# An attention and gating kernel: p v multiplies p's low part last, and z1 of the drain takes its PSUM banks from another pool

## The chip, the core and the metric

The kernel runs on one core of a Trainium2 chip. The metric is the device time of one execution in microseconds (us). Three executions of the kernel before took 1812.85, 1814.95 and 1819.16 us, so their median is 1814.95 us. One further execution was profiled. It took 1814.89 us, and its span from the first to the last instruction is 1813.1 us.

## What is computed

The reference, cut to what matters here (all of it in float32):

```
xn = layernorm(x)                                  # 2048 x 512
q  = (xn @ wq) as 32 heads of 128
s  = softmax(q @ k.T / sqrt(128)) @ v @ wo         # k, v: the last 512 cached rows of each head
z  = gelu(xn @ w_in)                               # 1376 columns: z1 is the first 688, z2 the rest
z2 = layernorm(z2)
g  = silu((z1 * (w_sp @ z2 + b_sp)) @ w_out)
out = x + s * g
```

Each product in it is made of three products: an operand a is held as a high part ah and a low part al = a - ah, both in the format float32r, and a b is computed as ah bh + ah bl + al bh, summed in PSUM.

## The kernel before

**Stages.** A short opening normalises the first rows and makes the first z1 products. Then comes the main loop (from about 50 to 1410 us of the span), which goes over 32 heads in two halves of the rows. After it a drain of some 40 us finishes the last blocks and makes the z1 products that are left. Then follow the z2 products, and from about 1510 us on the mixing by w_sp and the output projection.

**The main loop.** One block b is one head with 512 rows of x. It has four steps of 128 rows, so NBLK = 128 blocks make NSTEP = 512 steps. The work is software-pipelined by hand: in step t the code issues the scores of step t, the product p v of step t - 13 (PL, line 35 of the constants), and the output projection of step t - 18 (OL), along with the products for q of later blocks. The order in which the code issues instructions is the order on every engine, and each engine takes its own in that order.

For one step TensorE does this, in this order:

- the score (`score`, lines 470 to 479): three multiplications into a PSUM tile `ps_3` of the pool `ps_step`. VectorE takes its row maximum (line 477), and ScalarE the exponential (line 479). VectorE then turns p in pieces of 32 x 32 (line 488), and after four steps SyncE sends the block to DRAM and back (lines 492 and 500), which completes the transposition.
- the products for q (line 450), up to three of them, into `ps_a` of the pool `ps_acc`.
- p v (`pv`): p's transposed piece comes as `pT_h` and `pT_l` from `shares`. ScalarE makes the high part (line 507), and then GpSimd makes the low part by a subtraction (line 59, called in line 508). A block's four pieces are summed in one tile `ps_a`, which ScalarE and VectorE turn into `oT_h` and `oT_l` when the fourth is in (`pv_out`).
- the output projection (`outp`, lines 526 to 538): three multiplications into a `ps_3`, which VectorE adds to `sacc` (line 536).

`shares` runs two steps ahead of `pv`, and `pT_h` and `pT_l` have four buffers each. In the program's traces `wh` and `wl` are the high and low part of v (also of k and wo), and `ps` is `ps_3`.

The helper that issues three multiplications; the first operand is the one whose weights are loaded into the array:

```
    def mm3(ps, first, last, lhs, rhs):
        (lh, ll), (rh, rl) = lhs, rhs
        nc.tensor.matmul(ps, lh, rh, start=first, stop=False)      # line 65
        nc.tensor.matmul(ps, lh, rl, start=False, stop=False)      # line 66
        nc.tensor.matmul(ps, ll, rh, start=False, stop=last)       # line 67
```

In `pv` the first operand is v and the second is p. So the second multiplication, line 66, is the one that needs `pT_l`.

**The drain.** The z1 products of rows 8 to 15 (of 16 tiles of rows; T8 is 8) are spread over the last steps by the table DRAIN: first the eight with n = 0, at steps 505, 507, 509, 510, 511, 512, 513 and 514, then those with n = 1. Each is 12 multiplications of 344 columns, issued behind the step's output projection. ScalarE copies the result out of PSUM and issues its store to DRAM on its own queue (`z1_out`, lines 361 and 362). This copy's target has two buffers. In the drain the odd ones of the last subtractions for the split of w_in and for `pT_l` run on VectorE.

**PSUM.** There are eight banks. `ps_step` has four, named `ps_3`, and `ps_acc` has four, named `ps_a`. A new tile waits for the last reader of the tile that had its bank. Before, the z1 products with n = 0 take a `ps_3`, so scores, output projections and z1 share four banks; those with n = 1 take a `ps_a`.

**The SyncE queue.** SyncE issues nearly all DMAs, in the order of the code, and an issue that waits holds back those behind it. DMAs share eight semaphores. A DMA can be issued only when the one that had its semaphore before it has landed, whoever issued that one. In the drain this couples SyncE's loads with ScalarE's stores of z1. The loads of two blocks of x for the next stage (`fetch_x`, line 262, 1 MB each) stand there too.

Of the kernel before, what the change touches and what calls it, by code (L numbers as in the profile page):

```python
# [8 lines left out]
F32 = mybir.dt.float32  # L9
# [8 lines left out]
P = 128  # L18
# [16 lines left out]
T8 = NT // 2  # L35
# [5 lines left out]
def mixer_kernel(ctx: ExitStack, tc: tile.TileContext, x, wh, w_in, w_sp, b_sp, w_out, out):  # L41
# [8 lines left out]
    nc = tc.nc  # L50
# [12 lines left out]
    def mm3(ps, first, last, lhs, rhs):  # L63
        (lh, ll), (rh, rl) = lhs, rhs
        nc.tensor.matmul(ps, lh, rh, start=first, stop=False)  # L65
        nc.tensor.matmul(ps, lh, rl, start=False, stop=False)  # L66
        nc.tensor.matmul(ps, ll, rh, start=False, stop=last)  # L67

    def cols(pair, lo, hi):
        return tuple(t[:, lo:hi] for t in pair)  # L70
# [12 lines left out]
    ps_acc = psum.enter_context(tc.tile_pool(name="ps_acc", bufs=4, space=PSUM))  # L83
    ps_step = psum.enter_context(tc.tile_pool(name="ps_step", bufs=4, space=PSUM))
# [12 lines left out]
    raw, wt = {}, {}  # L97
# [241 lines left out]
    def zmm(ps, i, n, cs):  # L339
        for c in cs:  # L340
            mm3(ps, c == 0, c == NC - 1, tuple(x_op(i, a, c) for a in range(2)), cols(wt[("w", n), c], 0, NB))
# [8 lines left out]
                             start=k == 0, stop=k == len(order) - 1)  # L350

    def z1_product(i, n, between=lambda: None):
        ps = ps_acc.tile([P, 512], F32, name="ps_a") if n else ps_step.tile([P, 512], F32, name="ps_3")
        zmm(ps[:, :NB], i, n, range(2))
        between()
        zmm(ps[:, :NB], i, n, range(2, NC))
        return ps
# [6 lines left out]
    def z1_piece(i, n, between=lambda: None):  # L364
        z1_out(i, n, z1_product(i, n, between))


    qps, qT, pps, pD, pL, pT, oT, prob, sums = {}, {}, {}, {}, {}, {}, {}, {}, {}

    def where(b):  # L370

        w, r = divmod(b, NBLK // 2)
        p, k = divmod(r, 4)
        return w * H + 2 * p + k // 2, 2 * w + (0, 1, 1, 0)[k]
# [136 lines left out]
    def pv(b, c):  # L511
        if c == 0:
            pps[b] = ps_acc.tile([P, 512], F32, name="ps_a")
        mm3(pps[b], c == 0, c == 3, cols(wt[("h", where(b)[0]), 2], c * P, (c + 1) * P), pT.pop((b, c)))

    def pv_out(b, c):
        if c == 3:
# [85 lines left out]
    n, t = 0, 28  # L603
# [47 lines left out]
    ps = ps_step.tile([P, 512], F32, name="ps_3")  # L651
# [9 lines left out]
    ps = ps_step.tile([P, 512], F32, name="ps_3")  # L661
# [4 lines left out]
    ps = ps_acc.tile([P, 512], F32, name="ps_a")  # L666
# [18 lines left out]
    for t in range(T0, T1):  # L685
# [9 lines left out]
        i = t + XL  # L695
# [17 lines left out]
        if 0 <= bp < NBLK:  # L713
            pv(bp, cp)
        if 0 <= bo < NBLK:
            outp(bo, jo)
        if t in DRAIN:
            ps = z1_product(*DRAIN[t])
# [17 lines left out]

    split_piece(("w", 2), 3, nc.vector)
    ps = z1_product(*LAST[-1])
    split_piece(("w", 3), 1, nc.vector)
    z1_out(*LAST[-1], ps)  # L740
# [80 lines left out]
    with ExitStack() as st:  # L821
        pl = st.enter_context(tc.tile_pool(name="p2", bufs=1, reuse_waits="tile"))
# [193 lines left out]
```

## Time and profile before

| what | value |
|---|---|
| three timed executions | 1812.85, 1814.95, 1819.16 us |
| the profiled execution | 1814.89 us, span 1813.1 us |
| granted TensorE clock, mean | 0.998 |
| TensorE busy | 1793.2 us (99% of the span), 8658 multiplications |
| weight loads of TensorE | 1538.0 us (85%), 8658 |
| VectorE, ScalarE, GpSimd busy | 1395.4, 1174.4, 1237.8 us (77%, 65%, 68%) |
| DMA engines, main queue | 70.1% of 16 engines' span |

How to read the profile: PE is TensorE's multiplication and PEld its weight load, DVE is VectorE, ACT ScalarE, POOL GpSimd, SP SyncE. SPq and ACTq are DMA issues. A row of a timeline has the start in us, the duration in us, the engine, the line of the code, the operation, and output<-inputs; in brackets stands how long the engine was idle before it, and what ended that. Rows of multiplications overlap, since each is shown with its latency: the distance from start to start is what one costs. A view of waits has the waiting engine, its output tile and line, what it waited for, and then the us in total, the times, and the longest.

### The profile page before, as it was taken

How to read it: one execution, taken by the hardware profiler on the slowest of the kernel's cores; microseconds unless marked ns; L12 is line 12 of the kernel's file. 1: busy time of each engine (PE TensorE's matmuls, PEld its weight loads, DVE VectorE, ACT ScalarE, POOL GpSimd, SP SyncE). 2: the span in 40 equal slices, each digit the busy share in tenths (PEclk: the TensorE clock that was granted, in tenths of full speed). 3: DMA queues.
4: the chain of work that ended last, by engine and by line, in shares of the span. 5: the costliest groups of instructions: out<-in, count | busy, mean ns of one | idle time of the engine just before them, and what ended most of it. 6: DMA issues, size and time to landing. Idle time of an engine off the chain costs nothing.

```text
span 1813.1 us, 28712 instructions
## 1 busy us (share of the span) xinstructions
PE 1793.2 (99%) x8658; PEld 1538.0 (85%) x8658; DVE 1395.4 (77%) x2369; ACT 1174.4 (65%) x2625; POOL 1237.8 (68%) x1179
## 2 busy tenths in 40 slices
PE   8999999999999999999999999999999999999999
PEld 7887888888888888788888888888887999999998
DVE  5688988989898988888888888888888556433333
ACT  4777777777777777677777777777776444433332
POOL 2798898898888988788888888888887343000000
PEclk9999999999999999999999999999999999999999
DMA  5578887888888889787777777777778625554532
GB/s 181 176 226 249 245 252 236 266 251 232 253 254 248 250 248 303 256 256 226 232 219 223 219 230 221 225 235 218 226 224 253 219 86 172 171 172 148 182 118 92
DMA packets 181804, 394.07 MB, mean 217 GB/s; under 512 B 24368, under 2 KB 54832, under 8 KB 164496
## 3 DMA queue, kind: packets, MB, share of 16 engines
q1 hardware_dynamic: 177040, 386.60, 70.1%
q10 hardware_dynamic: 4608, 5.64, 0.9%
q8 instruction: 68, 1.11, 0.3%
q14 instruction: 88, 0.72, 0.1%
HBM read 225.42 MB, written 166.72 MB: 216 GB/s over the span
## 4 chain that ended last, share of the span: by engine, by line
PE 89%; DMA 6%; DVE 1%; ACT 1%; POOL 1%; issue 1%; SPq 1%; ACTq 0%; DVEq 0%; POOLq 0%
PE ps_a L450 14%; PE ps L67 12%; PE ps L65 12%; PE ps L66 12%; PE ps_a L66 7%; PE ps_a L67 7%; PE ps_a L65 7%; PE ps_g L65 4%; PE ps_g L67 4%; PE ps_g L66 4%; DMA p_dram<-pL 2%; DMA pL<-p_dram 1%; PE ps_f L67 1%; PE ps_f L65 1%; PE ps_f L66 1%
## 5 line engine op out<-in xcount | busy, mean ns | idle before, releaser
L59 POOL TENSOR_TENSOR pT_l<-pL,pT_h 128x512 fp32r<-128x512 f32 x507 | 656.5, 1298 | 187.6 <-ACT pT_h L507 155.4
L479 ACT ACTIVATE prob<-ps,nm 128x512 f32<-128x512 f32 x512 | 353.9, 691 | 330.4 <-DVE nm L477 320.8
L536 DVE SCALAR_TENSOR_TENSOR sacc<-ps,sums,sacc 128x512 f32<-128x512 f32 x496 | 369.6, 746 | 124.7 <-PE ps L67 118.8
L450 PE MATMUL ps_a<-x,x 128*128 128x512 f32 x1302 | 376.0, 389 | 1.0 <-DVE oT_l L59 1.0
L488 DVE STREAM_TRANSPOSE pL<-prob 128x512 f32<-128x512 f32 x512 | 358.7, 701 | 6.8 <-ACT prob L479 6.8
L477 DVE TENSOR_REDUCE nm<-ps 128x1 f32<-128x512 f32 x512 | 340.0, 664 | 7.0 <-PE ps L67 6.8
L507 ACT CAST pT_h<-pL 128x512 fp32r<-128x512 f32 x512 | 318.2, 622 | 28.1 <-DMA pL<-p_dram 7.6
L450 PEld LDWEIGHTS ps_a<-x,x 128*128 128x128 f32 x1302 | 244.4, 188 | 52.5 <-PE ps_a L450 1.8
L59 POOL TENSOR_TENSOR wl<-raw,wh 128x512 fp32r<-128x512 f32 x186 | 241.3, 1297 | 11.1 <-ACT wh L144 11.1
L66 PE MATMUL ps_a<-pT_l,wh 128*128 128x512 f32 x512 | 200.1, 391 | 3.0 <-POOL pT_l L59 2.8
L65 PE MATMUL ps_a<-pT_h,wh 128*128 128x512 f32 x512 | 199.5, 390 | 1.5 <-ACT pT_h L507 1.4
L65 PE MATMUL ps<-wh,qT_h 128*128 128x512 f32 x512 | 200.3, 391 | 0.5 <-DVE sacc L536 0.5
L67 PE MATMUL ps<-wh,qT_l 128*128 128x512 f32 x512 | 199.8, 390 | 0.0
L67 PE MATMUL ps_a<-pT_h,wl 128*128 128x512 f32 x512 | 199.3, 389 | 0.0
L66 PE MATMUL ps<-wl,qT_h 128*128 128x512 f32 x512 | 199.3, 389 | 0.0
L65 PE MATMUL ps<-wh,oT_h 128*128 128x512 f32 x512 | 199.3, 389 | 0.0
L66 PE MATMUL ps<-wl,oT_h 128*128 128x512 f32 x512 | 199.2, 389 | 0.0
L67 PE MATMUL ps<-wh,oT_l 128*128 128x512 f32 x512 | 199.2, 389 | 0.0
L67 PE MATMUL ps_g<-z_h,x 128*128 128x344 f32 x512 | 161.8, 316 | 0.0
L65 PE MATMUL ps_g<-z_h,x 128*128 128x344 f32 x512 | 161.8, 316 | 0.0
L66 PE MATMUL ps_g<-z_l,x 128*128 128x344 f32 x512 | 161.8, 316 | 0.0
L59 POOL TENSOR_TENSOR x<-wq,x 128x256 fp32r<-128x256 f32 x186 | 138.1, 743 | 1.5 <-ACT x L432 1.5
(203 smaller groups left out, 3179.4 us busy)
## 6 DMA issues: line engine op xcount, KB each, us to landing
p_dram<-pL SPq DMA_DIRECT2D x128, 1024.0 KB, 5.3
pL<-p_dram SPq DMA_DIRECT2D x256, 192.0 KB, 3.8
raw<-wh SPq DMA_DIRECT2D x188, 256.0 KB, 6.5
pL<-p_dram SPq DMA_DIRECT2D x256, 128.0 KB, 3.7
pL<-p_dram SPq DMA_DIRECT2D x256, 64.0 KB, 3.5
wq<-wh SPq DMA_DIRECT2D x62, 256.0 KB, 4.7
x<-w_sp SPq DMA_DIRECT2D x60, 256.0 KB, 5.7
x_dram<-rawx SPq DMA_DIRECT2D x32, 256.0 KB, 6.1
```

The source lines that it names most:

```text
L59: engine.tensor_tensor(lo, whole, hi.bitcast(F32), op=OP.subtract)
L65: nc.tensor.matmul(ps, lh, rh, start=first, stop=False)
L66: nc.tensor.matmul(ps, lh, rl, start=False, stop=False)
L67: nc.tensor.matmul(ps, ll, rh, start=False, stop=last)
L450: nc.tensor.matmul(qps[g, bank], wt["q", g, k][a][:, c * P:(c + 1) * P], X[g * 2 // H][ORDER[k]][:, b, c], start=first, stop=r == 5, skip_ ...
L477: nc.vector.tensor_reduce(nm, ps, axis=AX.X, op=OP.max, negate=True)
L479: nc.scalar.activation(prob[t], ps, AF.Exp, bias=nm, accum_out=sums[b][:, j:j + 1])
L488: nc.vector.transpose(pL[b][:, :, j * P:j * P + P].rearrange("p a (c q) -> p a c q", q=Q), prob.pop(t).rearrange("p (a c q) -> p a c q", a ...
L507: nc.scalar.copy(h, p)
L536: nc.vector.scalar_tensor_tensor(at, ps, rs, at, op0=OP.mult, op1=OP.add)
```

## The change

It has two parts. `pv` no longer calls `mm3`: it multiplies v high by p high, then v low by p high, then v high by p low, so that p's low part is needed by the third multiplication in place of the second. And `z1_product` takes a tile `ps_a` of `ps_acc` for n = 0 too, where the row tile is one of 8 to 15, that is, in the drain. The number of multiplications, weight loads and other instructions that compute is the same.

```
     def z1_product(i, n, between=lambda: None):
-        ps = ps_acc.tile([P, 512], F32, name="ps_a") if n else ps_step.tile([P, 512], F32, name="ps_3")
+        ps = ps_acc.tile([P, 512], F32, name="ps_a") if n or i >= T8 else ps_step.tile([P, 512], F32, name="ps_3")
...
     def pv(b, c):
         if c == 0:
             pps[b] = ps_acc.tile([P, 512], F32, name="ps_a")
-        mm3(pps[b], c == 0, c == 3, cols(wt[("h", where(b)[0]), 2], c * P, (c + 1) * P), pT.pop((b, c)))
+        (vh, vl), (ph, pl) = cols(wt[("h", where(b)[0]), 2], c * P, (c + 1) * P), pT.pop((b, c))
+        nc.tensor.matmul(pps[b], vh, ph, start=c == 0, stop=False)
+        nc.tensor.matmul(pps[b], vl, ph, start=False, stop=False)
+        nc.tensor.matmul(pps[b], vh, pl, start=False, stop=c == 3)
```

On TensorE a step of the main loop then stands as follows (the piece of the difference with the waits of each; `ps_a` is first the accumulator of q, then that of p v, `wh_811` and `wl_812` are v's parts):

```order
 L450 MATMUL ps_a<-x_508,x_751 128x512 x3
-L65 MATMUL ps_a<-pT_h,wh_811 128x512 [waits Activation_49]
-L66 MATMUL ps_a<-pT_l,wh_811 128x512 [waits Pool_49]
-L67 MATMUL ps_a<-pT_h,wl_812 128x512
+L515 MATMUL ps_a<-pT_h,wh_811 128x512 [waits Activation_49]
+L516 MATMUL ps_a<-pT_h,wl_812 128x512
+L517 MATMUL ps_a<-pT_l,wh_811 128x512 [waits Pool_49]
 L65 MATMUL ps_1012<-wh_747,qT_h 128x512
```

The wait for GpSimd's `pT_l` moved behind one more multiplication; nothing else on TensorE moved in the step.

On GpSimd the order stays, but waits change. A piece of its list of subtractions in the main loop:

```order
-L59 TENSOR_TENSOR pT_l<-pL,pT_h 128x512 [waits Activation_49]
+L59 TENSOR_TENSOR pT_l<-pL,pT_h 128x512 [waits PE_49,Activation_49]
 L59 TENSOR_TENSOR wl_1183<-raw,wh_1182 128x512 [waits DMAHW5_49,Activation_49]
 L59 TENSOR_TENSOR pT_l<-pL,pT_h 128x512 [waits PE_49,Activation_49]
 L423 TENSOR_TENSOR wq<-wq 128x256 [waits Pool_49]
 L59 TENSOR_TENSOR pT_l<-pL,pT_h 128x512 [waits PE_49,Activation_49]
-L59 TENSOR_TENSOR wl_1254<-raw,wh_1253 128x512 [waits DMAHW4_49,PE_49,Activation_49]
+L59 TENSOR_TENSOR wl_1254<-raw,wh_1253 128x512 [waits DMAHW4_49,Activation_49]
```

`pT_l`'s old content is now read by the last multiplication of p v, so a subtraction that before needed no wait of its own for TensorE has one. That is so for 182 of the 507, and in 155 places the wait is an instruction of its own; 60 subtractions `wl` lose such a wait.

In the drain, TensorE's list around step 509: the step's output projection (tile 17625), its z1 product (tile 17630), and the score of step 510 (tile 17660). Before:

```order
L65 MATMUL ps_3_17625<-wh3_17282,oT_h_17453 128x512 [waits Activation_49]
L66 MATMUL ps_3_17625<-wl3_17283,oT_h_17453 128x512
L67 MATMUL ps_3_17625<-wh3_17282,oT_l_17454 128x512
L65 MATMUL ps_3_17630<-x8_17180,x8_8451 128x344 [waits DVE_49]
...
L65 MATMUL ps_3_17660<-wh1_17312,qT_h_17366 128x512 [waits Activation_49]
```

And of the change:

```order
L65 MATMUL ps_3_17625<-wh3_17282,oT_h_17453 128x512 [waits Activation_49]
L66 MATMUL ps_3_17625<-wl3_17283,oT_h_17453 128x512
L67 MATMUL ps_3_17625<-wh3_17282,oT_l_17454 128x512
L65 MATMUL ps_a_17630<-x8_17180,x8_8451 128x344
...
L65 MATMUL ps_3_17660<-wh1_17312,qT_h_17366 128x512 [waits DVE_49]
```

The z1 product has no wait any more. The wait for VectorE is now at the score of the next step, and it is the same one: both tiles wait until VectorE has added the output projection of step 508 (tile 17594) to `sacc`, since both get its bank. On SyncE one more thing differs in the drain, since the order in which DMAs share the eight semaphores shifts. Of the first two loads of line 262, the first waited for a load of `pL` and the second for the landing of a z1 store that ScalarE had issued; in the changed program the first waits for the z1 store before that one, and the second for a load of `pL`.

## The prediction

> **What bounds the kernel now.** I read the page first, for which engine is full.
>
> ```profile
> span 1813.1 us, 28712 instructions
> PE 1793.2 (99%) x8658; PEld 1538.0 (85%) x8658; DVE 1395.4 (77%) x2369; ACT 1174.4 (65%) x2625; POOL 1237.8 (68%) x1179
> PE 89%; DMA 6%; DVE 1%; ACT 1%; POOL 1%; issue 1%; SPq 1%; ACTq 0%; DVEq 0%; POOLq 0%
> ```
>
> TensorE is busy 99% of the span and carries 89% of the chain that ended last. Neither part of the change takes a multiplication away, so the change can only give back time in which TensorE stands still: 1813.1 - 1793.2 = 19.9 us in all, much of it in the opening, which the change does not touch. What it waits for is in the view of waits, for the multiplications and for the weight loads ahead of them:
>
> ```profile
> PE ps_a L66 <- POOL pT_l L59: 2.8, 4, 0.8
> PE ps L65 <- DVE sacc L536: 2.1, 3, 1.6
> ...
> PEld ps_a L66 <- POOL pT_l L59: 6.4, 9, 1.3
> ```
>
> The first and the last row are the waits at which the new order of p v aims: nine times in 512 pieces the low part came too late for its weight load, and four of these left the multiplier idle by the profile. The second row holds one long wait of 1.6 us; the timeline below puts it on a z1 product. So before any detail the two parts have something like 2.8 to 6.4 us and 1.6 us to work on, 0.2 to 0.4% of the time.
>
> The price of one multiplication comes from a stretch of the timeline without a wait, first and last of nine in a row:
>
> ```profile
> 1396.92 0.39 PE L65 MATMUL ps<-wh,qT_h 128*128 128x512 f32 x1
> ...
> 1398.74 0.39 PE L67 MATMUL ps<-wh,oT_l 128*128 128x512 f32 x1
> ```
>
> Eight distances take 1398.74 - 1396.92 = 1.82 us, 0.2275 us each.
>
> **Part 1: p's low part last.** Where the low part is late at TensorE, 0.2275 us of work that does not need it is now done in the meantime. So an episode of waiting shrinks by at most 0.2275 us, and nine episodes give at most 2.05 us. But what one episode gives need not last. The first five lie close together:
>
> ```profile
> 77.90 0.19 PEld L66 LDWEIGHTS ps_a<-pT_l,wh 128*128 128x128 f32 x1 [0.48 <-POOL pT_l L59]
> ...
> 93.34 0.19 PEld L66 LDWEIGHTS ps_a<-pT_l,wh 128*128 128x128 f32 x1 [0.49 <-POOL pT_l L59]
> 76.50:95.90 19.40, 18.10 (x74) 13.28 (x74) 15.21 (x27) 14.32 (x34) 19.22 (x18) 1.00 0.83 255
> 95.90 0.62 ACT L507 CAST pT_h<-pL 128x512 fp32r<-128x512 f32 x1 [2.72 <-DMA pL<-p_dram]
> 101.05 0.19 PEld L450 LDWEIGHTS ps_a<-x,x 128*128 128x128 f32 x1 [0.56 <-PE ps_a L450]
> ```
>
> The third row is one of the table by stretches; its columns are the length of the stretch and the busy time of PE, PEld, DVE, ACT and POOL: GpSimd works 19.22 of 19.40 us. Its subtractions end when they end, and TensorE meets the last of them at 93.34 whatever it gained at the first. So these five give 0.2275 us together, not five times that. The last row shows TensorE waiting again at 101.05, now for a bank; its release goes through ScalarE, which the row ahead of it shows waiting 2.72 us for a DMA until 95.90. If that DMA is no earlier, the 0.2275 us are given back there. The later episodes look alike:
>
> ```profile
> 734.48 0.19 PEld L66 LDWEIGHTS ps_a<-pT_l,wh 128*128 128x128 f32 x1 [1.15 <-POOL pT_l L59]
> 741.12 0.19 PEld L65 LDWEIGHTS ps<-wh,qT_h 128*128 128x128 f32 x1 [0.21 <-ACT qT_h L384]
> 741.85 0.19 PEld L67 LDWEIGHTS ps<-wh,qT_l 128*128 128x128 f32 x1 [0.43 <-DVE qT_l L59]
> ```
>
> Here the low part stalls TensorE for 1.15 us, and 7 us later the parts of q do, which hang on ScalarE and not on TensorE's lead. A lead lasts only where every later wait is paced by TensorE itself, as a transfer that it started earlier. There are four such groups (77 to 93, 142.7, 734.5 and 1385.8 us), so part 1 gives between 0 and 4 x 0.2275 = 0.9 us by this reading, 2.05 us if no episode's gain is lost. I take 0.2 us, one group's worth, nearest to the rows that show it given back.
>
> What it adds: 182 subtractions on GpSimd now wait for TensorE, 155 of them by an instruction of its own. The buffer in question was read two steps earlier, so that wait is over when it is asked. Its price in GpSimd's queue is read from a `wl`, which has such extra waits already, behind a `pT_l`:
>
> ```profile
> 79.23 1.29 POOL L59 TENSOR_TENSOR pT_l<-pL,pT_h 128x512 fp32r<-128x512 f32 x1
> 80.47 1.29 POOL L59 TENSOR_TENSOR wl<-raw,wh 128x512 fp32r<-128x512 f32 x1
> 81.72 0.74 POOL L59 TENSOR_TENSOR x<-wq,x 128x256 fp32r<-128x256 f32 x1
> ```
>
> It starts 1.24 us after the `pT_l`, and the `x` behind it 1.25 us later: back to back either way. I take 0. The upper end is 0.05 us, the hop from VectorE's end at 1400.66 to TensorE's start at 1400.72 in the rows further down; that is 0.25 us for the five episodes in the full stretch and nothing elsewhere, since GpSimd is 68% busy. It would only eat part 1's gain.
>
> One rule speaks against the new order. The Trainium skill's page "TensorE: Matmul & The Clock Gate", section "Step-by-step: what each phase is for", says that weights are loaded apart from multiplying so that one load can serve many multiplications. By that rule the old order, with v's high part twice in a row, needs two loads for three multiplications, and the new one three. The page's row above has 8658 loads for 8658 multiplications, so the old order loads it again as well.
>
> **Part 2: z1 of the drain.** The wait of 1.6 us has this chain, rows of ScalarE, VectorE and TensorE in the order of time; the first two are an earlier z1 product, which waits for nothing, and the score behind it:
>
> ```profile
> 1393.05 0.32 PE L65 MATMUL ps<-x,x 128*128 128x344 f32 x1
> ...
> 1394.88 0.39 PE L65 MATMUL ps<-wh,qT_h 128*128 128x512 f32 x1
> ...
> 1396.67 0.33 ACTq L362 DMA_DIRECT2D z_dram<-z  x1
> 1397.57 0.47 ACT L144 CAST x<-rawx 128x344 fp32r<-128x344 f32 x1
> 1398.08 1.33 DVE L59 TENSOR_TENSOR x<-rawx,x 128x344 fp32r<-128x344 f32 x1 [3.46 <-ACT x L144]
> 1399.33 0.68 DVE L477 TENSOR_REDUCE nm<-ps 128x1 f32<-128x512 f32 x1
> 1399.93 0.73 DVE L536 SCALAR_TENSOR_TENSOR sacc<-ps,sums,sacc 128x512 f32<-128x512 f32 x1
> 1400.72 0.43 PE L65 MATMUL ps<-x,x 128*128 128x344 f32 x1 [1.59 <-DVE sacc L536]
> 1402.72 0.39 PE L65 MATMUL ps<-wh,qT_h 128*128 128x512 f32 x1
> ```
>
> ScalarE's store of an earlier z1 was held until 1396.67, VectorE stood idle for 3.46 us behind it, and so it emptied the output projection's bank only at 1399.93 + 0.73 = 1400.66. The z1 product of step 509 needed that bank. TensorE's last multiplication before it started at 1398.74, so without the wait the z1 product starts at 1398.74 + 0.23 = 1398.97. Twelve multiplications of 344 columns take 1402.72 - 1400.72 = 2.00 us in this execution but 1394.88 - 1393.05 = 1.83 us in the first two rows, where nothing waits. So they end at 1398.97 + 1.83 = 1400.80. What is late next: the score of step 510 now waits for the very release that z1 waited for, at 1400.66, which is when its weights are wanted. The hop of 0.06 us to 1400.72 costs it hardly anything; I put it at 1400.82. It started at 1402.72, so part 2 gives 1402.72 - 1400.82 = **1.9 us**. Bounds: 0, if the wait moves on whole, and 2.1 us, if the other waits of that row (2.1 - 1.6 = 0.5 us) go too, of which the nearest to 1.9 is what the rows sum to.
>
> ```profile
> 1403.00:1455.00 52.00, 52.00 (x288) 47.68 (x287) 27.20 (x43) 23.25 (x50) 16.34 (x15) 1.00 0.70 233
> ```
>
> This row of the table by stretches shows that TensorE had no gap from 1403 to 1455 us. Is there slack for it to come 1.9 us earlier? The transfers that feed p there are held by the z1 stores, which follow TensorE and move with it. So I let the whole 1.9 us reach the end; the stages behind have no wait that the profile shows for TensorE.
>
> **Sum.** 1.9 + 0.2 = 2.1 us. The profiled execution took 1814.89 us, which lies 0.06 us under the median of the three, so the forecast is 1814.9 - 2.1 = **1812.8 us**, 0.12% faster. A measurement of this kernel can tell about 0.3% (5.4 us) from no change, and the three runs are 6.3 us apart, so this counts as the same.
>
> **The rivals.** (a) Part 1's gains all last, because the transfers start earlier too: 1814.9 - 1.9 - 2.05 = 1810.9 us. For it speaks that the chain has only 6% of DMA; against it the rows at 101.05 and 741.12. (b) The stall of the drain comes back elsewhere. It starts with a landing that took long: the z1 store ahead of the held one landed only 7.0 us after its issue, where the median of these stores is 2.9:
>
> ```profile
> z_dram<-z ACTq DMA_DIRECT2D x1, 172.0 KB, 7.0
> z_dram<-z ACTq DMA_DIRECT2D x32, 172.0 KB, 2.9
> ```
>
> If it lands a microsecond or two later in another execution, the score of step 510 waits for it in full, and if it lands soon there was no stall to remove. Either way: 1814.9 - 0.2 = 1814.7 us. (c) Slower: the second load of 1 MB at line 262 starts together with the first one instead of 8 us behind it, and both crowd a z1 store.
>
> ```profile
> SPq L262 <- DMA z_dram<-z: 7.9, 1, 7.9
> z_dram<-z ACTq DMA_DIRECT2D x1, 172.0 KB, 7.8
> 1431.76 0.33 ACTq L362 DMA_DIRECT2D z_dram<-z  x1
> 1439.67 0.45 ACT L361 COPY z<-ps_a 128x344 f32<-128x344 f32 x1 [1.96 <-DMA z_dram<-z]
> 1440.52 0.62 ACT L507 CAST pT_h<-pL 128x512 fp32r<-128x512 f32 x1 [0.41 <-ACT z L361]
> 1443.40 0.39 PE L65 MATMUL ps_a<-pT_h,wh 128*128 128x512 f32 x1
> ```
>
> The store issued at 1431.76 landed 7.8 us later, at 1439.56, beside one such load. ScalarE waits for it before the next copy of z1, and ends the last block's `pT_h` at 1440.52 + 0.62 = 1441.14, 1.6 us after the landing. TensorE wants it at 1443.40, or 1.9 us earlier now, at 1441.50, and the store goes out at 1429.86. So it decides at a landing of 1441.50 - 1.6 - 1429.86 = 10.0 us. If two loads double the landing to 15.6 us, TensorE waits 5.6 us there: 1814.9 - 2.1 + 5.6 = 1818.4 us, slower. Against it: one more store, issued beside two such loads, landed in 7.6 us.
>
> ```profile
> 1452.52 0.33 ACTq L362 DMA_DIRECT2D z_dram<-z  x1
> x<-x_dram SPq DMA_DIRECT2D x2, 1024.0 KB, 6.5
> z_dram<-z ACTq DMA_DIRECT2D x1, 172.0 KB, 7.6
> ```
>
> The Trainium skill's page "DMA: Bandwidth & Descriptors", section "Queues, rings and completion order", says that a DMA engine goes round the queues that have work, a packet at a time; by that rule a store on ScalarE's queue is not put behind a second load on SyncE's, and the forecast stands. The two landings, 7.8 and 7.6 us, agree with it. (d) Weights that stand in the array already are cheap, so that the new order pays one weight load more for each of 512 pieces, at most 188 ns each (96 us): 1911 us. The equal counts of loads speak against it, and so do the equal distances within the nine multiplications above, in which a load of the same weights and of new ones alternate.
>
> **How the numbers follow.** Forecast 0.57, (a) 0.14, (b) 0.18, (c) 0.10, (d) 0.01. The predicted time is the forecast's, 1812.8 us. The cases (a) to (c) span 1810.9 to 1818.4 us, and the three runs lie from 2.1 us under their median to 4.2 us over it; a median of runs moves by about half of that. So the range is 1809.3 to 1818.4 us. Faster by over 0.3% (under 1809.5 us) needs (a) and a low draw: 0.06. Slower by over 0.3% (over 1820.4 us) needs (c) and a high draw, or (d): 0.06. The same: 0.88.
>
> **What would show it.** Part 1: the row of PEld waiting for `pT_l` (now at line 517) falls from 6.4 us by some 0.2 us an episode and does not vanish, and bank waits do not shrink. Part 2: TensorE's wait of 1.6 us for VectorE before a z1 product is gone, the score behind it starts at most 0.1 us late, and the drain is 1.9 us shorter from the z1 product of step 509 on. (b) would show as a wait of a score for VectorE of over 1 us in the drain, (c) as a wait of p v for ScalarE near 1441 us, (d) as distances over 0.2275 us at lines 515 to 517. Wrong I would be if another wait grew that the profile of before does not hold, as one of GpSimd for TensorE.

## The result, and the profile after

The changed kernel took **1813.65 us** (median of 19 executions, 1811.26 to 1816.47); the kernel before, beside it, 1816.28 us (19 executions, 1812.85 to 1821.64). The ratio is 0.9986, with a 95% interval of 0.9980 to 0.9992: faster by 1.5 to 3.6 us, 0.14%, and under the 0.3% within which the prediction counts a time as the same. The forecast was 1812.8 us, 0.12% under the profiled execution; that execution, at 1814.89 us, was itself 1.4 us under the median that before has now.

The page of the changed kernel, its span, its engines and its chain:

```profile
span 1810.6 us, 28863 instructions
PE 1793.3 (99%) x8658; PEld 1539.5 (85%) x8658; DVE 1395.6 (77%) x2369; ACT 1173.4 (65%) x2625; POOL 1237.7 (68%) x1179
PE 93%; DMA 4%; DVE 1%; POOL 1%; issue 1%; ACT 0%; SPq 0%; ACTq 0%; POOLq 0%; DVEq 0%
```

TensorE is as busy as before (1793.3 us), in a span that is 2.5 us shorter. The 151 more instructions are the waits on GpSimd (155 more, and a few fewer elsewhere), and GpSimd's busy time did not move. TensorE carries 93% of the chain in place of 89%, transfers 4% in place of 6%. The view of waits, weight loads, two rows of the change and one of before:

```profile
PEld ps_a L517 <- POOL pT_l L59: 4.7, 7, 1.3
PEld ps L65 <- DVE sacc L539: 2.1, 5, 0.8
```

```profile
PEld ps L65 <- DVE sacc L536: 3.6, 4, 2.0
```

The waits for `pT_l` fell from 6.4 to 4.7 us and those of a score or z1 for VectorE from 3.6 to 2.1 us. That looks like 1.7 + 1.5 us, and like the forecast. But only the second number stands up.

**The drain.** Timeline of the changed kernel around the z1 product of step 509, ScalarE's first two stores of the drain ahead of it:

```profile
1388.79 0.33 ACTq L362 DMA_DIRECT2D z_dram<-z  x1
1396.09 0.33 ACTq L362 DMA_DIRECT2D z_dram<-z  x1
1397.92 0.39 PE L67 MATMUL ps<-wh,oT_l 128*128 128x512 f32 x1
1398.15 0.32 PE L65 MATMUL ps_a<-x,x 128*128 128x344 f32 x1
...
1399.84 0.31 PE L67 MATMUL ps_a<-x,x 128*128 128x344 f32 x1
1400.12 0.19 PEld L65 LDWEIGHTS ps<-wh,qT_h 128*128 128x128 f32 x1 [0.25 <-DVE sacc L539]
1400.13 0.50 PE L65 MATMUL ps<-wh,qT_h 128*128 128x512 f32 x1
```

The second store went out 7.30 us behind the first, 0.08 us after the first had landed (1396.01); in before it was 7.07 us. The z1 product no longer feels it: it starts 0.23 us behind the last multiplication of the output projection. The score of step 510 now waits for VectorE, and it starts 1400.13 - 1399.84 = 0.29 us behind the last z1 multiplication in place of 0.15: 0.14 us late. Behind the drain the execution is 1.7 us further ahead of before than it was ahead of the drain.

**The main loop.** Start of the same multiplication of TensorE, in before, and how much earlier (-) or later it starts in other executions, worked out from their timelines (us):

| mark in before | 29.0 | 61.3 | 95.3 | 157.0 | 731.3 | 750.6 | 1380.7 | 1407.3 | last, 1808.7 |
|---|---|---|---|---|---|---|---|---|---|
| before, second profile | -1.0 | -1.0 | -0.7 | -2.7 | -2.0 | -0.6 | -0.6 | -1.1 | -1.1 |
| the change | +0.8 | +0.8 | +0.9 | -2.1 | -2.0 | -0.8 | -0.8 | -2.5 | -2.5 |
| the change, second profile | +0.6 | +0.6 | +1.1 | +0.5 | +0.6 | +2.5 | +2.5 | +0.5 | +0.5 |

Between 95 and 157 us the change gains 2.9 us and at 731 to 751 us it loses 1.3 us, and neither belongs to it: at the first place its own second profile gains 0.6 us, and the second profile of *before* gains 2.0; at the second all three lose, by 1.3 to 2.0 us, and in all three, but not in the first profile of before, TensorE's clock was halved for a while there (last section). Only the step from 1380.7 to 1407.3 us is the same wherever the banks are changed: -1.7 and -2.0, against -0.5 for the kernel before against itself. So the 2.5 us between the two profiled executions, so close to the 2.1 of the forecast, are a sum of terms of up to 3 us that cancelled by chance.

### The profile page after: what moved, and what is told of

Same layout as the page of the kernel before. It is cut to its first block, busy times and chain, and to the rows that moved or that the text cites. A ratio compares the mean times of both kernels' runs of the same rounds, so it can differ in the third digit from the quotient of the medians.

```text
span 1810.6 us, 28863 instructions
## 1 busy us (share of the span) xinstructions
PE 1793.3 (99%) x8658; PEld 1539.5 (85%) x8658; DVE 1395.6 (77%) x2369; ACT 1173.4 (65%) x2625; POOL 1237.7 (68%) x1179
## 4 chain that ended last, share of the span: by engine, by line
PE 93%; DMA 4%; DVE 1%; POOL 1%; issue 1%; ACT 0%; SPq 0%; ACTq 0%; POOLq 0%; DVEq 0%
PE ps_a L450 15%; PE ps L65 12%; PE ps L67 12%; PE ps L66 12%; PE ps_a L517 6%; PE ps_a L515 6%; PE ps_a L516 6%; PE ps_g L67 4%; PE ps_g L66 4%; PE ps_g L65 4%; PE ps_a L67 2%; PE ps_a L66 2%; PE ps_a L65 2%; DMA p_dram<-pL 1%; DMA pL<-p_dram 1%; PE ps_f L67 1%
```

## The experiments

Ratios are to runs of the kernel before on the same chip, with 95% intervals. They are not the quotients of the two medians, from which they differ by up to 0.0009. Each run was also profiled once.

**1. `order_only`: the new order of p v, the old banks** (the change without its first edit).

> Only the new order of p v, the drain as before. Theory of the prediction: an episode of waiting for pT_l shrinks by up to 0.2275 us and most of that is given back at the next wait, so about 0.2 us less than before (ratio 0.9999), the wait of 1.6 us of the z1 product at 1400 us stays, the pT_l waits of PEld fall from 6.4 to about 4.7 us. Rival: all gains last, 2.05 us less (ratio 0.9989). Second rival, from the trace of the change: TensorE is 2.0 us ahead of before at 146 us, so the order would be worth some 2.9 us there by starting transfers of p earlier.

Measured: 1816.97 us against 1816.03, ratio 1.0004 (0.9992 to 1.0017). Waits of this kernel, and its timeline in the drain:

```profile
PEld ps_a L517 <- POOL pT_l L59: 7.4, 10, 1.3
```

```profile
1390.32 0.35 ACTq L362 DMA_DIRECT2D z_dram<-z  x1
1395.81 0.45 ACT L361 COPY z<-ps 128x344 f32<-128x344 f32 x1 [1.09 <-PE ps L67]
1396.28 0.33 ACTq L362 DMA_DIRECT2D z_dram<-z  x1
1400.33 0.43 PE L65 MATMUL ps<-x,x 128*128 128x344 f32 x1 [0.48 <-DVE sacc L539]
```

The order alone has more waiting for `pT_l` than before (7.4 us, ten times), not less: three episodes came in, near 166, 720 and 723 us, that before does not have. The lower end of the interval, -1.5 us, excludes rival (a) with its 2.05 us, and the second rival with its 2.9 us too. This profile does gain 2.4 us between 95 and 157 us, but `before_again` and `low_first`, with other orders, gain 2.0 us there. And the stall of z1 is here, but with 0.48 us in place of 1.59. The second store was not held at all: the first had landed at 1395.83, and the second went out right behind its copy (1395.81 + 0.45 = 1396.26), 5.96 us behind the first. So part of the stall needs no late landing.

**2. `banks_only`: the new banks, the old order.**

> Only the z1 banks of the drain, p v's order as before. Theory of the prediction: the wait of 1.6 us before the z1 product of step 509 is gone, the score behind it waits at most 0.1 to 0.2 us, 1.9 us less than before (ratio 0.9990). Rival: the wait moves to the score, 0 us (ratio 1.000).

Measured: 1814.43 us against 1816.03, ratio 0.9991 (0.9980 to 1.0002), so the timing alone does not tell it from no change. In the trace the stall is gone: with the stores 1402.76 - 1396.16 = 6.60 us apart the z1 product follows the output projection by 0.23 us.

```profile
1396.16 0.33 ACTq L362 DMA_DIRECT2D z_dram<-z  x1
1402.76 0.34 ACTq L362 DMA_DIRECT2D z_dram<-z  x1
...
1405.30 0.39 PE L67 MATMUL ps<-wh,oT_l 128*128 128x512 f32 x1
1405.53 0.32 PE L65 MATMUL ps_a<-x,x 128*128 128x344 f32 x1
```

One wait is new, and it is close to rival (c), but small: p v of the last block waits 0.24 us, behind a `pT_h` for which ScalarE had waited 2.34 us until 1438.68. That wait was for a load of `pL`, which landed at 1438.54 beside the two loads of 1 MB issued at 1436.29 and 1436.77, and not for a z1 store. Weight loads of the same run:

```profile
1440.71 0.19 PEld L66 LDWEIGHTS ps_a<-pT_l,wh 128*128 128x128 f32 x1 [0.50 <-POOL pT_l L59]
```

**3. `low_first`: the dose the other way.** p's low part first, old banks:

```
-        mm3(pps[b], c == 0, c == 3, ...)
+        nc.tensor.matmul(pps[b], vh, pl, start=c == 0, stop=False)
+        nc.tensor.matmul(pps[b], vh, ph, start=False, stop=False)
+        nc.tensor.matmul(pps[b], vl, ph, start=False, stop=c == 3)
```

> The dose the other way: p's low part is multiplied first, so it is needed one multiplication sooner than before. If every episode's time counts in full, each of the nine grows by 0.2275 us and others join them: at least 2.05 us more than before (ratio at least 1.0011), pT_l waits of PEld at least 8.4 us. If the time is mostly given back at the next wait, the waits grow as much but the time by some 0.2 to 1 us (ratio up to 1.0005).

Measured: 1817.13 us against 1816.03, ratio 1.0004 (0.9993 to 1.0016). Its waits:

```profile
PEld ps_a L515 <- POOL pT_l L59: 9.5, 11, 3.0
```

The waits grew by 3.1 us over before, but one of them, 3.0 us at the half's boundary, now holds the wait for `pT_h` too. The time is compatible with either reading; the first group, below, is not.

**4. `low_late`: a larger dose.** For c < 3 the multiplication vh pl is kept in a list and issued behind the step's output projection (old banks).

> A larger dose: for three of a block's four pieces the low part is multiplied behind the output projection, four or more multiplications (0.9 us) later than before. Waits for pT_l should nearly vanish (under 2 us of PEld's 6.4). If their time is kept, 4 to 5 us less than before (ratio 0.997 to 0.998). If what paces these stretches is GpSimd's own work and the landing of p's transfers, the waits turn into waits for banks, pT_h or q and the time falls by under 2 us (ratio 0.999 to 1.000).

Measured: 1813.93 us against 1816.03, ratio 0.9990 (0.9978 to 1.0001).

```profile
PEld ps_a L518 <- POOL pT_l L59: 3.4, 4, 1.3
```

Less waiting, but not "nearly none". The expectation overlooked that steps 13 to 17, where most of the first group lies, have no output projection yet, so the dose there is that of the change. The time cannot be told from no change.

**5. `store_pool`: no hold of ScalarE.** The kernel before, with the z1 stores of the drain issued by GpSimd:

```
-        nc.scalar.dma_start(z1_dram[:, i, n * NB:(n + 1) * NB], z)
+        (nc.gpsimd if i >= T8 else nc.scalar).dma_start(z1_dram[:, i, n * NB:(n + 1) * NB], z)
```

> The kernel before (old order, old banks), but GpSimd's queue issues the z1 stores of the drain, so that ScalarE's queue is not held until the store ahead has landed. Theory: that hold makes the stall of the z1 product at step 509; in the four profiles with the old banks the stall is the time between ScalarE's first two stores of the drain less 5.3 us (7.07 gives 1.75, 6.70 gives 1.42, 6.49 gives 1.23, 5.96 gives 0.64). Without the hold it is gone (under 0.1 us) with the old banks too, and the time falls like that of the new banks alone, by 1.2 to 1.6 us (ratio 0.9991 to 0.9994). Rival: the stall belongs to the four banks shared by three users and stays near 1.3 us, ratio 1.000.

Measured: 1815.56 us against 1816.23, ratio 1.0002 (0.9993 to 1.0010). The timeline, with the old banks:

```profile
1396.53 0.45 ACT L361 COPY z<-ps 128x344 f32<-128x344 f32 x1 [1.06 <-PE ps L67]
...
1397.28 0.56 POOL L362 DMA_DIRECT2D z_dram<-z  x1 [0.52 <-PE ps L67]
1397.39 0.48 ACT L144 CAST x<-rawx 128x344 fp32r<-128x344 f32 x1
1397.91 1.64 DVE L59 TENSOR_TENSOR x<-rawx,x 128x344 fp32r<-128x344 f32 x1 [1.85 <-ACT x L144]
...
1400.07 0.73 DVE L536 SCALAR_TENSOR_TENSOR sacc<-ps,sums,sacc 128x512 f32<-128x512 f32 x1
...
1400.86 0.43 PE L65 MATMUL ps<-x,x 128*128 128x344 f32 x1 [0.29 <-DVE sacc L536]
```

The hold is gone, and the stall fell to 0.45 us (start to start, less one multiplication), not under 0.1. What is left has the same chain without a transfer in it: ScalarE's cast for `x` stands behind its copy of z1, which waits for the z1 product itself; VectorE waits 1.85 us for the cast, and empties the bank late. So the expected gain of 1.2 to 1.6 us did not come; the interval reaches from 1.3 us less to 1.8 us more. Part of what the shorter stall saves goes to GpSimd: its issue of a store holds its queue for 0.56 us here, and two waits for `pT_l` in the drain cost TensorE 0.49 and 0.40 us, where before had one of 0.19 us.

```profile
1382.57 0.50 PE L66 MATMUL ps_a<-pT_l,wh 128*128 128x512 f32 x1 [0.33 <-POOL pT_l L59]
1387.21 0.50 PE L66 MATMUL ps_a<-pT_l,wh 128*128 128x512 f32 x1 [0.24 <-POOL pT_l L59]
```

**6. `banks_low_next`: the change with the dose of a whole step.** For c < 3, vh pl is issued in the next step, ahead of its p v.

> The change with a larger dose: for three of a block's four pieces the low part is multiplied a whole step later (2.7 us). Waits for pT_l of these pieces vanish (2.1 us of idle TensorE between 77 and 95 us in before and in the change alike, and about 1 us at the half's boundary near 734 us). If their time is kept, 3 us less than the change, ratio to before 0.997. If the landing of p's transfers paces these stretches, a wait for pT_h or a bank follows within 10 us, and at most 1 us is gained over the change, ratio 0.998 to 0.9986.

Measured: 1814.36 us against 1816.23, ratio 0.9991 (0.9980 to 1.0002), no better than the change. The wait for `pT_l` from 74 to 96 us is 1.2 us of weight loads in place of 3.4, and these came in its place (timeline; lines behind 62 are one higher in this kernel):

```profile
91.03 0.50 PE L66 MATMUL ps<-wh,qT_h 128*128 128x512 f32 x1 [0.50 <-ACT qT_h L385]
...
98.08 0.47 PE L451 MATMUL ps_a<-x,x 128*128 128x512 f32 x1 [0.34 <-DVE oT_l L59]
```

A wait for q's high part, which in before shows only at 741 us, and one for a bank. At 95.3 us TensorE is 0.4 us ahead, counted from 61 us, where the waits that were taken away come to 1.5 us.

**7. `relief`: four subtractions to VectorE.** The change, with the low parts of pieces 1, 3, 5 and 7 on VectorE.

> The change, and in addition the low parts of pieces 1, 3, 5 and 7 of p are subtracted by VectorE instead of GpSimd (5.2 us less for GpSimd between 77 and 95 us). Theory: GpSimd's own work makes the first group of waits for pT_l, so these 2.1 us of idle TensorE go to under 0.5 us; of that a part comes back at the next wait for a landing near 96 to 101 us, so 0.5 to 1.5 us less than the change, ratio to before 0.9978 to 0.9984. Rival: they stay, since GpSimd waits for the transfers of p anyway, ratio 0.9986.

Measured: 1814.29 us against 1816.23, ratio 0.9990 (0.9981 to 0.9999), the same as the change. The expectation failed: TensorE fell 3.1 us behind between 61 and 95 us. Waits of VectorE from 74 to 100 us:

```profile
DVE pT_l L59 <- ACT pT_h L507: 4.2, 4, 1.4
```

A subtraction that stands in VectorE's queue before its `pT_h` is there holds the row maxima and additions behind it, and with them scores and projections. Those 3.1 us were given back in full by 157 us (-0.2, as at 61 us).

**8. `relief_early`: three subtractions earlier.** The change, with three splits `wl` of the weights made 3, 3 and 4 steps earlier on GpSimd.

> The change, and in addition three of the subtractions wl that stand between those of pT_l on GpSimd (at 77.81, 80.47 and 84.90 us in the trace of before) are made 3, 3 and 4 steps earlier, where GpSimd is idle for 5.8 us between 69 and 77 us. No engine gets more work. Theory: the first group of waits for pT_l is GpSimd's own work, so its 2.1 us go to under 0.5 us; with a smaller wait for the landing of p's transfers behind it, TensorE is 1.5 to 2 us ahead of the change at 95 us, and 0.5 to 1.5 us of it are left at the end, ratio to before 0.9978 to 0.9984. Rival: waits for pT_h, q or banks take the same time, as in the run with the low part a step later, and the ratio stays at 0.9986.

Measured: 1814.04 us against 1815.03, ratio 0.9986 (0.9973 to 0.9999), the same as the change. GpSimd now waits where it was full, and TensorE still does (timeline):

```profile
85.06 1.28 POOL L59 TENSOR_TENSOR pT_l<-pL,pT_h 128x512 fp32r<-128x512 f32 x1 [2.09 <-ACT pT_h L507]
86.39 0.50 PE L517 MATMUL ps_a<-pT_l,wh 128*128 128x512 f32 x1 [0.62 <-POOL pT_l L59]
...
99.58 0.47 PE L450 MATMUL ps_a<-x,x 128*128 128x512 f32 x1 [0.53 <-DVE oT_l L59]
```

Of the change's four episodes the longest (1.02 us) is gone, and 1.5 us are left where under 0.5 were expected. The one at the first piece of the second block stays, since GpSimd waits 2.09 us for it: it is paced by the landing of p. Counted from 61 us and against before, TensorE is 0.4 us ahead at 95.3 us and 0.1 us at 122.7 us. The rival holds, as far as a profile and an interval of 2.4 us either way can tell.

**9. `before_again`: the same kernel once more.**

> The kernel before once more, for its profile: nothing is changed. If the 2.9 us that TensorE gains between 95 and 157 us in the trace of the change come from its order, this profile is within 0.5 us of the first one at every mark. If they come from transfers that land at other times in each execution, it differs by 1 to 3 us at 157 us and again near 734 us.

Its row in the table above differs by 2.0 us between 95 and 157 us, as the second reading has it. A cause there, ScalarE's wait for p:

```profile
138.01 0.62 ACT L507 CAST pT_h<-pL 128x512 fp32r<-128x512 f32 x1 [2.50 <-PE ps_a L65]
```

In the first profile of before the same cast came at 140.66, 4.34 us after the one ahead had ended, in the first of the change at 138.09 after 1.27 us. The view names TensorE as the releaser; but TensorE had read that buffer some steps before, while the loads of `pL` issued from 124 to 140 us took 7.3 to 8.8 us to land here and 5.6 to 6.6 us in the change (medians by size). So it is put down to the landing, which no run took away by itself.

**10. `after_again`: the change once more.**

> The change once more, for a second profile. Theory: the same as the first in what the program decides (four or five waits for pT_l of 2.1 us in sum between 77 and 95 us, and a drain of 24.5 to 24.9 us from the score of step 504 on, against 25.4 to 26.6 with the old banks), and different by 1 to 3 us where transfers decide (near 140 us and near 734 us).

It waits 0.51, 1.02, 0.70 and 0.21 us for `pT_l` between 77 and 95 us (2.4 in all), its drain takes 24.6 us, and it lacks the 2.9 us, with a bank wait in their place that the first profile did not have. At the half's boundary the two differ by 0.7 us only (losses of 1.3 and 2.0 us), less than was expected:

```profile
141.12 0.62 ACT L507 CAST pT_h<-pL 128x512 fp32r<-128x512 f32 x1 [3.20 <-DMA pL<-p_dram]
...
146.30 0.47 PE L450 MATMUL ps_a<-x,x 128*128 128x512 f32 x1 [1.02 <-DVE oT_l L59]
```

**11 and 12. The banks alone and the change, side by side.**

> The z1 banks alone once more, timed beside the whole change. Theory: the drain alone makes the gain, 1.4 us by the traces (ratio 0.9992), and the order of p v adds 0.1 to 0.2 us, so the two medians are within 1 us of each other. Rival: the order is worth 1 us or more in combination, so this run is at least 1 us slower than the one beside it.

> The whole change once more, beside the z1 banks alone. Theory: 1.5 us less than before (ratio 0.9992), the same as the banks alone within 1 us. Rival: 2.6 us less than before (ratio 0.9986) and 1 us or more under the banks alone.

Measured on one chip, against 1816.53 us: the banks alone 1814.53 us (ratio 0.9994, 0.9984 to 1.0003), the change 1814.02 us (0.9988, 0.9979 to 0.9997). They are 0.5 us apart, within the 1 us of the theory, though each interval is wider than that.

## Why the prediction was right, and where

**Part 2, the mechanism: shown.** Over the thirteen profiles in which ScalarE issues the stores, the time between its first two stores of the drain (called the hold here), and how much later than its distance without a wait TensorE starts the z1 product of step 509 (old banks) or the score behind it (new banks):

| old banks | hold us | z1 late by us | hold less lateness | | new banks | hold us | score late by us |
|---|---|---|---|---|---|---|---|
| `order_only` | 5.96 | 0.64 | 5.32 | | `relief_early`, `banks_low_next` | 5.96 | 0 |
| `low_first` | 6.49 | 1.23 | 5.26 | | `after_again` | 6.53 | 0 |
| `before_again` | 6.59 | 1.30 | 5.29 | | `banks_only`, `after_second`, `relief` | 6.59, 7.01, 7.12 | 0 |
| `low_late` | 6.70 | 1.42 | 5.28 | | `banks_second` | 7.20 | 0.04 |
| before | 7.07 | 1.75 | 5.32 | | the change | 7.30 | 0.14 |

In ten of the thirteen the second store went out 0.07 or 0.08 us after the first had landed, so there a landing set the hold. In the three with 5.96 us the first had landed 0.29 to 1.72 us before, and the hold is only the distance of the two copies of z1. So with the old banks 0.64 us of the stall come from the order of work alone, and a late landing adds up to 1.1 us.

With the old banks every microsecond of hold above 5.3 us is a microsecond of TensorE. With the new ones it begins at 7.30 - 0.14 = 7.20 - 0.04 = 7.16 us: 1.9 us later, which is the z1 product (1.83 us) that now stands ahead of the wait. That is the step "the score of step 510 now waits for the very release that z1 waited for, at 1400.66, which is when its weights are wanted", to 0.1 us.

**Part 2, the size: 1.9 us was too much.** The one profile on which it rested had the longest hold of five. From 1380.7 to 1407.3 us of before, TensorE took 26.59, 26.05, 25.43 and 26.06 us with the old banks (before twice, `order_only`, `low_first`: mean 26.0) and 24.59 to 24.85 us in seven profiles with the new ones and p v's multiplications within their step (mean 24.7). Two of these seven have the old order of p v (24.63 and 24.85 us), and do not stand apart. So the banks give **1.3 to 1.4 us**. It adds up: the z1 product is late by 1.23 us in the mean of the four, and its twelve multiplications take 0.15 us longer behind a wait. What was mis-sized is the term of 1.9 us, by the unsaid step that this landing is the same in each execution. Rival (b) had the right doubt ("if it lands soon there was no stall to remove"), but put it as all or nothing: in `order_only` the store landed in time and z1 was still 0.64 us late.

**Part 1: about 0.2 us, as forecast, and it cannot be timed.** In the first group, the lateness of the multiplications of `pT_l` from 75 to 95 us, less what GpSimd itself stood idle ahead of the first piece of the second block (by 84 to 88 us, where p lands late):

| order | waits less GpSimd's idle time, us | mean |
|---|---|---|
| low part first (one profile) | 2.36 - 0 | 2.36 |
| low part second, as before | 2.12 - 0, 2.13 - 0, 3.04 - 0.92, 2.43 - 0.27, 2.82 - 0.60 | 2.15 |
| low part last | 2.12 - 0.14, 2.23 - 0.24, 2.44 - 0.48, 1.99 - 0 | 1.98 |

One place in the order is worth 0.17 to 0.21 us for the *whole group*, not for each of its five episodes: "these five give 0.2275 us together" was right. The reason given, that GpSimd's subtractions end when they end, shows in GpSimd's own rows, the first and the seventh subtraction of p, of before:

```profile
76.55 1.30 POOL L59 TENSOR_TENSOR pT_l<-pL,pT_h 128x512 fp32r<-128x512 f32 x1 [1.75 <-DMA wq<-wh]
...
91.99 1.29 POOL L59 TENSOR_TENSOR pT_l<-pL,pT_h 128x512 fp32r<-128x512 f32 x1
```

and of the change, timed beside the banks alone:

```profile
77.68 1.29 POOL L59 TENSOR_TENSOR pT_l<-pL,pT_h 128x512 fp32r<-128x512 f32 x1 [1.75 <-ACT pT_h L507]
...
93.15 1.29 POOL L59 TENSOR_TENSOR pT_l<-pL,pT_h 128x512 fp32r<-128x512 f32 x1
```

15.44 and 15.47 us. The added waits on GpSimd, for which 0 was taken, are hardly tested by this: in this full stretch its queue has 12 wait instructions in place of 11. So one more of them costs at most 0.03 us; for the rest, GpSimd's busy time did not move.

**What was to show it, and did not.** "The row of PEld waiting for `pT_l` falls from 6.4 us by some 0.2 us an episode" was a bad test. The row gave 4.7, 5.5 and 4.6 us in the three profiles of the change, 7.4 for the same order alone, and 6.2 to 9.3 in the five with p v as before: which pieces wait outside the first group changes from one profile of the same kernel to the next.

**The rivals.** (a) fell with `order_only`, and with `banks_low_next` and `relief_early`: taking more of these waits away, by a larger dose or at their cause, gained nothing over the change that the timing shows, and in the traces waits for q, for banks and for landings stand behind them. (c): its condition came true. In the change the two loads of line 262 start at 1428.38 and 1428.86, and the store issued at 1429.25 held ScalarE's copy until 1437.36, so it landed in at most 8.1 us, against the 10.0 that decide. Near the two loads p v lost time in two profiles, 0.24 us in `banks_only` and 0.31 us in `low_first`, each time behind a load of `pL` and not behind a store. (d): the three multiplications of p v in the new order, in a stretch without a wait, are 0.23 and 0.22 us apart:

```profile
120.52 0.39 PE L515 MATMUL ps_a<-pT_h,wh 128*128 128x512 f32 x1
120.75 0.39 PE L516 MATMUL ps_a<-pT_h,wl 128*128 128x512 f32 x1
120.97 0.39 PE L517 MATMUL ps_a<-pT_l,wh 128*128 128x512 f32 x1
```

So new weights cost no more than the same again here, and (d) falls.

**Luck.** The time came out 0.9 us above 1812.8 us. The base, the median of three executions, lay 1.4 us under the median of nineteen, and the measured gain is 0.5 us larger than the 2.1 us of the forecast; the two errors partly cancel.

**What stays open.** The traces account for 1.4 + 0.2 = 1.6 us, the timed medians differ by 2.6 (interval 1.5 to 3.6) and by 2.5 in the run beside the banks alone. The banks alone came out 1.6 and 2.0 us faster by their medians, but neither interval is clear of no change, so that they make the gain is shown by the traces and not by the timing. Whether the missing microsecond is noise, or a gain at landings that shifts on average, these runs do not tell.

## What to carry to other kernels

A wait whose length is set by a transfer's landing has a different size in each execution, so a forecast from one profile should take its price from the relation (lateness = hold - 5.3 us here), from the least that the hold can be (5.96 us) and from a spread of holds, and a second profile of the *same* kernel is the cheapest experiment there is. Where a full engine feeds TensorE over many steps, a reordering that hides one multiplication's time hides it once for the whole stretch, not once per episode. And a wait that is given to the next user of the bank is gone only by as much work as now stands ahead of it.

## What was not expected of the hardware

**A pause of TensorE may be followed by half speed.** At the half's boundary it waits for p. In the change its clock was then halved; the table by stretches shows 0.53 as granted clock from 733.0 to 736.5 us, and the timeline multiplications 0.43 us apart:

```profile
733.00:736.50 3.50, 3.50 (x10) 2.67 (x10) 2.32 (x4) 2.91 (x9) 3.50 (x5) 0.53 0.53 194
```

```profile
732.70 0.67 PE L517 MATMUL ps_a<-pT_l,wh 128*128 128x512 f32 x1 [0.62 <-POOL pT_l L59]
733.16 0.63 PE L65 MATMUL ps<-wh,oT_h 128*128 128x512 f32 x1
733.59 0.63 PE L66 MATMUL ps<-wl,oT_h 128*128 128x512 f32 x1
```

From 732.70 to 736.68 us the multiplications take 1.6 us more than at full clock. It came in 11 of the 14 profiles, after the opening at no other place. In the first profile of before the same stretch kept its full clock, in its second it did not, so it isn't the change. The length of the pause does not decide it alone: `store_pool` waited longer and stayed at full clock, 0.23 us apart.

```profile
733.61 0.50 PE L65 MATMUL ps_a<-pT_h,wh 128*128 128x512 f32 x1 [2.38 <-ACT pT_h L507]
...
735.52 0.39 PE L65 MATMUL ps<-wh,oT_h 128*128 128x512 f32 x1
735.75 0.39 PE L66 MATMUL ps<-wl,oT_h 128*128 128x512 f32 x1
```

The Trainium skill's page "TensorE: Matmul & The Clock Gate", section "What's actually happening", says that the clock falls to half after an idle window of about 3.4 us, and that the windows run freely. That they run freely agrees with a pause that is punished in one execution and not in the next; the idle times here are shorter than such a window (1.65 us, and 0.62 us after two multiplications, in the change), so the row differs from the page in the length that it takes.
